# Batch 1's queries turned by VectorE and SyncE instead of TensorE, and the first unit of a fused attention-and-MLP kernel laid out anew

## The chip, the cores and the metric

The kernel runs on one core of a Trainium2 chip. The metric is the device time of one execution in microseconds. The kernel before took 898.84 us, the median of three runs (898.73, 898.84, 899.49). All data is float32.

## What is computed

Eight batches of attention, with eight heads, 576 queries and a head width of 64. Keys and values are averaged over groups of eight first, so each head has 72 keys. The result, 4608 tokens of 512 columns, goes through a two-layer network with a periodic activation between the layers:

```python
k_p = k.reshape(B, H, Sp, pool, D).mean(axis=3)          # pool = 8, Sp = 72
v_p = v.reshape(B, H, Sp, pool, D).mean(axis=3)
scores = scale * np.matmul(q, k_p.transpose(0, 1, 3, 2))
scores = scores - np.max(scores, axis=-1, keepdims=True)
attn = np.exp(scores)
attn = attn / (np.sum(attn, axis=-1, keepdims=True) + 1e-09)
x = np.matmul(attn, v_p)                                 # -> (4608, 512)
h = x @ w_in                                             # 512 x 2048
s = np.sin(alpha * h)
g = h + s * s / (alpha + 1e-09)
out = g @ w_out                                          # 2048 x 512
```

## The kernel before

**Stages.** The order of all instructions is written out by hand: what the program issues first on an engine runs first on it. First comes batch 0's attention (`first_batch`, L1105), which leaves the activations of the first 512 tokens in SBUF. Then the hidden layer runs in nine units `u` of 512 tokens (`hidden(u, extra)`, L835). Last comes the second layer (`outputs`, L1317, its products at L1383; the first of them start at 504.7 us, the hidden layer's last product at 510.9). The activated hidden values go from the one to the other through an internal DRAM tensor, `g_bridge`.

**A unit and its slots.** A unit has 28 slots: four groups J = 0 to 3 of output columns, each with seven products k = 0 to 6 (a Strassen scheme with seven products instead of eight, in the order 1, 5, 6, 2, 7, 3, 4). Slot number = 7J + k. One product is four matmuls of 128x256, which the trace shows as eight records at L866. Around each product the slot issues that group's share of the elementwise work: copies on ScalarE (L839), additions on VectorE (L838), sines and squares on ScalarE (`sin` L1028, `square` L1035), the last additions of the group before (`finish`, L1080) and the store of its result (`store_g`, L1091).

**Work hung on slots.** `carry(u)` (L1202) builds the list `extra`: `at(slot, f, ...)` appends a step to a slot. These steps are the attention of batch u+1, loads, and sums of weights, and they are issued between the unit's own instructions. Steps at "slot - 0.5" are issued at the start of the slot; those of a whole slot number at a fixed place inside it, mostly right ahead of its product. Unit 0 has a list of its own, because at that time batch 0's last tile is unfinished, w_in is still being loaded in four parts (`load_w_in_part`, L677; sums of each part by `combine_w_in`, L684), and q, k and v of batch 1 have just been requested.

**Batch 1's attention in unit 0, before.**
- `load_k` (L117) loads k of one half of the heads, with one run of 6 KB for each partition; `pool_rows` (L128) adds groups of eight on GpSimd (L132). `first_batch` issues k, then q of batch 1 (`load_q(1)`), then w_in's part 1; slot 2 issues w_in's parts 2 and 3.
- q: ScalarE puts heads into pairs (`pairs_q`, L88 to L98, slots 2 and 3). TensorE transposes five tiles of it, four transposes each (`q_t`, L282, transposes L290, slots 4, 4, 8, 8, 9), and VectorE or ScalarE copies them out of PSUM (L291). `k_t` (L274, slot 4) transposes the pooled k on TensorE.
- `two_scores` (L304, matmuls L318, slots 6 and 11): scores of query tiles 0 and 1, then of 2 and 3 with the last 64 rows. VectorE subtracts the row maximum (L341, L342), ScalarE takes the exponential (L366, slots 9, 9, 15, 15), `norm` (L369, slots 10, 10, 16, 16) has VectorE sum and invert the sums, and GpSimd multiply (L375).
- `turn` (L498, transposes L504, slots 13, 13, 19, 19): VectorE transposes the weights of attention in 32x32 blocks into the tile `tr`. `move` (L517, L524, slot 19) then carries bands of 32 partitions of `tr` to other partitions, into the tile `aM`, by DMA. There are four blocks of two halves of two transfers, 16 in all; before, SyncE issues the 12 of blocks 0 to 2 and ScalarE's queue the 4 of block 3.
- `all_values` (slot 26, matmuls L613) multiplies `aM` with the pooled values. Its first matmuls read the second halves of all four blocks of `aM`.

**Later batches' q, before.** `turn_q` (L216) has four parts. In parts 0 and 1 VectorE transposes q in 32x32 blocks into `tr` (L229, L234). In parts 2 and 3 SyncE issues eight moves each (L244), from bands of `tr` back into q's tile. For batch 2 the four parts stand in slots 23 to 26 of unit 0, and `tr` is the same buffer that the attention weights use. In the trace this tile is called `q` and the moves are `q<-tr`.

**Batch 0's last tile.** Its 64 rows finish in unit 0: `exp(4)` slot 9, `norm_rest` slot 13, `a_rest` (transposes) slot 21, `values_rest` (L626) slot 24.

**Queues.** SyncE issues nearly all transfers, in program order, and waits at each for what it needs. A DMA that waits holds back all later ones of SyncE. The end of J = 2's group in unit 0 is finished at slots 24 and 26 (`finish(Q, (0,))`, `finish(Q, (1,))`, `store_g`).

Of the kernel before, what the change touches and what calls it, by code (L numbers as in the profile page):

```python
# [13 lines left out]
F32 = mybir.dt.float32  # L14
# [26 lines left out]
class Kernel:  # L41
# [46 lines left out]
    def pairs_q(self, b, tiles):  # L88

        nc = self.nc  # L90
        if 0 in tiles:
            self.raw = self.q_views(self.qm[b])
            self.qm[b] = self.q_tile(1)
        x = self.qm[b][:].rearrange("p (t h e d) -> p t e h d", t=5, e=2, d=self.D)
        for t in tiles:
            n = P if t < 4 else 64
            raw = self.raw[0][:, :, t, :] if t < 4 else self.raw[1]
            nc.scalar.copy(out=x[:n, t], in_=raw.rearrange("p (e h) d -> p e h d", e=2))  # L98

    def load_q_rest(self, b, at=None):  # L100
        if b < 2:
            self.nc.sync.dma_start(out=self.q_views(self.qm[b])[1] if at is None else at, in_=self.q[b, :, 4 * P:, :].rearrange("h p d -> p h d"))
# [14 lines left out]
    def load_k(self, b, e):  # L117

        Sp, D, NP = self.Sp, self.D, self.NP
        m = Sp // 3  # L120
        t = self.kvp.tile([P, 2048], F32, name="kvin")[:NP * m, 0:3 * POOL * D]
        self.nc.sync.dma_start(out=t, in_=self.k[b, NP * e:NP * e + NP].rearrange("h (p x) d -> (h p) (x d)", x=3 * POOL))
        if b not in self.kp:
            self.kp[b] = self.ap.tile([NP * m, 3, 2, D], F32, name="kp")
        t, out = t.rearrange("p (j x) -> p j x", j=3), self.kp[b][:, :, e, :]
        self.pool_k[e] = lambda: self.pool_rows(t, out)
# [132 lines left out]
    def attention(self, b):  # L259
# [22 lines left out]
        def q_t(i, copy=nc.scalar.copy):  # L282

            n = rows[i]
            x = self.qm[b][:n].rearrange("p (t hp x) -> p t hp x", t=5, hp=NP)[:, i]
            if b not in self.qt:
                self.qt[b] = self.qt_view(self.q_tile(0))
            ps = self.abank([P, NP, P])
            for hp in range(NP):
                nc.tensor.transpose(ps[:, hp, :n], x[:, hp], self.ident[:n, :n])  # L290
            copy(out=self.qt_tiles(b)[:, i, :, :n], in_=ps[:, :, :n])  # L291

        def columns(hp, i):

            if b < 2:
# [73 lines left out]
        def norm(i):  # L369

            n = E(i).shape[1]
            sm = self.sm.tile([P, 12], F32, name="sm2")[:, 0:n]
            nc.vector.tensor_reduce(out=sm, in_=E(i, Sp + 1), axis=AX, op=OP.add)
            nc.vector.reciprocal(out=sm, in_=sm)
            nc.gpsimd.tensor_tensor(out=E(i), in0=E(i), in1=sm.unsqueeze(2).to_broadcast([P, n, Sp]), op=OP.mult)  # L375
# [150 lines left out]
        def to_x(ps, hp, t0, m, s0=0):  # L526

            while s0 < m:
# [5 lines left out]
                if t0 and b > 1:  # L534
# [8 lines left out]
        def value_parts(hp, rest):  # L543
# [14 lines left out]
            order = lambda x: x.rearrange("p a (t i) -> p t a i", i=32) if b == 1 else x  # L558
            at = lambda r, n, h: order(self.aM[r:r + n, :, 128 * h:128 * h + 128])
# [74 lines left out]
        return SimpleNamespace(**{f.__name__: f for f in (k_t, q_t, products, score, two_scores, two_shifts, exp, norm, new_a, turn, move, values, values_rest, all_values,  # L634
# [200 lines left out]
    def hidden(self, u, extra):  # L835
# [41 lines left out]
        for slot in range(7 * self.NJ):  # L877
# [6 lines left out]
            for f in extra[slot - 0.5]:  # L884
                f()

            if k == 0:
                Q = self.before = G
# [15 lines left out]
            elif k == 1:  # L904
                if not G.i1:
                    copy(G.b6[:], G.b1[:])
                if G.i5 and not G.i1:
                    self.last_sines(Q, 0)
                elif Q and not G.i1:
                    if end(J):  # L910
                        self.last_sines(Q, 2)
# [5 lines left out]
            elif k == 2:  # L917
                if Q and not G.i5 and not split(J):
# [20 lines left out]
            elif k == 3:  # L939
                late = J == 0 and busy  # L940
                if Q and not late and not G.i5 and not split(J):
# [11 lines left out]
                else:  # L953
# [11 lines left out]
                    extras()  # L965
                    product(G, 2, G.b1)
# [19 lines left out]
            elif k == 5:  # L986
                add(G.g[:, 1, :, 1], G.b7[:], G.p5[:])
                extras()
                if split(J):
                    self.finish(Q, (1,))  # L990
                    self.store_g(Q)
# [8 lines left out]
            else:  # L1000
# [3 lines left out]
                sin(G, 1, 1, G.g[:, 1, :, 1])  # L1004
# [100 lines left out]
    def first_batch(self):  # L1105
# [88 lines left out]
        self.load_w_in_part(0, ((2, 1, 0),))  # L1194
        for e in range(2):
            self.load_k(1, e)
            self.pool_k[e]()
        self.combine_w_in(0, (3,), nc.gpsimd)
        self.load_q(1)
        self.load_w_in_part(1)  # L1200

    def carry(self, u):  # L1202
# [6 lines left out]
        if u == 0:  # L1209
# [9 lines left out]
            at(2, self.load_w_in_part, 3)  # L1219
            at(2, self.pairs_q, 1, (0, 1))  # L1220
            at(3, self.pairs_q, 1, (2, 3, 4))
            at(4, self.combine_w_in, 1, (0, 1, 2, 3), self.nc.gpsimd)
            at(4, A.q_t, 0, self.nc.vector.tensor_copy)
            at(4, A.q_t, 1, self.nc.vector.tensor_copy)
            at(4, A.k_t)
            at(7, self.load_v, 1)
            at(7, lambda: self.pool_v())
            for i in range(2):
                at((6, 11)[i], A.two_scores, i)
            at(13, A.two_shifts)  # L1230
# [482 lines left out]
```

## Time and profile before

| | us |
|---|---|
| device time, median of 3 | 898.84 |
| profiled execution, first to last instruction (span) | 896.15 |
| hidden layer's last product starts (L866) | 510.86 |
| TensorE busy | 890.8 (99%) |
| VectorE busy | 682.9 (76%) |
| ScalarE busy | 438.6 (49%) |
| GpSimd busy | 249.2 (28%) |

The page gives the busy time of each engine over the span (PE is TensorE, DVE VectorE, ACT ScalarE, POOL GpSimd, SP SyncE; SPq marks a row of DMA issues by SyncE). Its second part cuts the span into 40 slices of 22.4 us, with busy shares in tenths; the two that matter here are the second and third (22 to 67 us), where nearly all of unit 0 lies:

```
POOL 6798443825338252434523000000000000000000
PEclk9999999999999999999999999999999999999999
DMA  9857957759586585648126243716435355164002
GB/s 269 244 158 206 244 147 212 187 164 254 139 ...
```

The granted TensorE clock is full in all slices. In the timeline a row is a run of equal instructions: its start, its length (for a pipelined engine from the first start to the last end), engine, line, operation, output <- inputs, shapes and count, and in brackets the idle time of the engine before it with what ended that. In unit 0 the rows of TensorE follow each other without such a bracket; slot 6 (the first scores) starts at 35.66, slot 11's scores at 47.14, slot 26's values at 76.32, and unit 1's first scores at 89.08.

### The profile page before, as it was taken

To read this page: it belongs to the slowest core of one execution; us is meant where nothing else is said; L and a number is where in the kernel's file an instruction comes from. 1 tells how busy PE (TensorE), PEld (TensorE's weight loads), DVE (VectorE), ACT (ScalarE), POOL (GpSimd) and SP (SyncE) were. 2 spreads that over 40 slices of the span, in tenths; PEclk is the share of its full clock that TensorE was granted. 3 is DMA by queue.
4 is the path that set the end of the run, shared out by engine and by line. 5 is a ranking of instruction groups with operands and counts; after the bars stand their busy time and mean duration, and the time that the engine had idled before them with its cause. 6 is when DMAs were issued, how large, how long until landed. Compare 5 with 4: busy or idle time off the path is not lost.

```text
span 896.2 us, 16276 instructions
## 1 busy us (share of the span) xinstructions
PE 890.8 (99%) x6274; PEld 813.9 (91%) x6274; DVE 682.9 (76%) x918; ACT 438.6 (49%) x1033; POOL 249.2 (28%) x265
## 2 busy tenths in 40 slices
PE   9999999999999999999999999999999999999998
PEld 6787888888888888888888999999999999999998
DVE  7786857768577675765677889898897896996885
ACT  6687776877768777687776711111111211111111
POOL 6798443825338252434523000000000000000000
PEclk9999999999999999999999999999999999999999
DMA  9857957759586585648126243716435355164002
GB/s 269 244 158 206 244 147 212 187 164 254 139 214 186 183 225 147 175 140 302 53 106 219 102 181 103 232 37 218 117 105 160 89 159 159 37 192 142 20 18 53
DMA packets 119533, 141.03 MB, mean 157 GB/s; under 512 B 45776, under 2 KB 86496, under 8 KB 119456
## 3 DMA queue, kind: packets, MB, share of 16 engines
q1 hardware_dynamic: 116288, 137.39, 52.6%
q10 hardware_dynamic: 3168, 2.61, 1.0%
q8 instruction: 50, 0.82, 0.4%
q14 instruction: 27, 0.22, 0.1%
HBM read 75.37 MB, written 47.19 MB: 137 GB/s over the span
## 4 chain that ended last, share of the span: by engine, by line
PE 99%; DVE 0%; POOL 0%; ACT 0%; issue 0%; DVEq 0%
PE PS L866 44%; PE PS L1383 43%; PE PS L1058 5%; PE PS L318 2%; PE PS L613 2%; PE PS L626 1%; PE PS L1126 0%; PE PS L571 0%; PE PS L290 0%; PE PS L425 0%; PE PS L279 0%; PE PS L479 0%; PE PS L569 0%; POOL tr L451 0%; PE PS L403 0%; PE PS L487 0%
## 5 line engine op out<-in xcount | busy, mean ns | idle before, releaser
L866 PE MATMUL PS<-home,a 128*128 128x256 f32 x1072 | 253.0, 381 | 0.1
L866 PEld LDWEIGHTS PS<-home,a 128*128 128x128 f32 x1072 | 198.4, 190 | 30.9 <-issue 4.6
L866 PE MATMUL PS<-home,as 128*128 128x256 f32 x736 | 177.2, 382 | 0.0
L866 PEld LDWEIGHTS PS<-home,as 128*128 128x128 f32 x736 | 134.5, 190 | 18.1 <-ACT PS L839 1.2
L1383 PE MATMUL PS<-s,wb 128*128 128x192 f32 x672 | 116.2, 326 | 0.0
L1035 ACT ACTIVATE s<-s,c 128x256 f32<-128x256 f32 (+1 forms) x236 | 115.5, 556 | 0.0
L1383 PEld LDWEIGHTS PS<-s,wb 128*128 128x128 f32 x672 | 110.4, 190 | 0.1
L132 POOL TENSOR_TENSOR kvin<-kvin 96x768 f32<-96x768 f32 (+3 forms) x42 | 73.4, 1747 | 69.9 <-DMA kvin<-in_v_dram 67.8
L838 DVE TENSOR_TENSOR h<-PS,p 128x512 f32<-128x512 f32 x72 | 49.2, 684 | 55.5 <-PE PS L866 35.2
L1554 ACT COPY PS<-PS 128x192 f32<-128x192 f32 x42 | 12.7, 303 | 146.2 <-PE PS L1383 130.0
L1028 ACT ACTIVATE s<-h,al 128x256 f32<-128x256 f32 x144 | 65.5, 509 | 32.6 <-DVE h L838 32.6
L1383 PE MATMUL PS<-r,wb 128*128 128x192 f32 x432 | 79.0, 326 | 0.0
L1383 PEld LDWEIGHTS PS<-r,wb 128*128 128x128 f32 x432 | 71.6, 190 | 0.0
L1383 PE MATMUL PS<-s,a 128*128 128x192 f32 x384 | 70.2, 326 | 0.0
L1028 ACT ACTIVATE s<-PS,al 128x256 f32<-128x256 f32 x144 | 60.0, 469 | 17.2 <-PE PS L866 16.5
L1383 PEld LDWEIGHTS PS<-s,a 128*128 128x128 f32 x384 | 63.7, 190 | 0.0
L1080 DVE TENSOR_TENSOR h<-PS,s 128x512 f32<-128x512 f32 x36 | 24.8, 689 | 48.6 <-ACT s L1035 48.6
L839 ACT COPY PS<-PS 128x512 f32<-128x512 f32 x72 | 41.5, 577 | 34.5 <-PE PS L866 26.7
L1080 DVE TENSOR_TENSOR h<-h,s 128x1024 f32<-128x1024 f32 x36 | 55.3, 1537 | 3.3 <-ACT s L1035 3.1
L1584 ACT COPY PS<-PS 128x192 f32<-128x192 f32 x42 | 12.7, 303 | 89.5 <-PE PS L1383 89.5
L1322 DVE TENSOR_TENSOR s<-r 128x768 f32<-128x768 f32 x54 | 51.4, 951 | 4.8 <-PE PS L1383 2.8
L1383 PE MATMUL PS<-s,we 128*128 128x192 f32 x288 | 52.7, 326 | 0.0
(244 smaller groups left out, 1401.4 us busy)
## 6 DMA issues: line engine op xcount, KB each, us to landing
g_bridge<-h SPq DMA_DIRECT2D x72, 512.0 KB
r<-g_bridge SPq DMA_DIRECT2D x15, 1536.0 KB
x<-g_bridge SPq DMA_DIRECT2D x8, 1536.0 KB
out_dram<-o SPq DMA_DIRECT2D x90, 96.0 KB
kvin<-in_k_dram SPq DMA_DIRECT2D x14, 576.0 KB
q<-in_q_dram SPq DMA_DIRECT2D x7, 1024.0 KB
kvin<-in_v_dram SPq DMA_DIRECT2D x14, 512.0 KB
aM<-tr SPq DMA_DIRECT2D x54, 92.0 KB
```

The lines of the kernel that those rows point to most:

```text
L132: self.nc.gpsimd.tensor_tensor(out=t[..., 0:w] if w > D else out, in0=t[..., 0:w], in1=t[..., w:2 * w], op=OP.add)
L318: nc.tensor.matmul(ps[e][r0 + r:r0 + r + q.shape[-1], h, :], q[s], kb[s, hp, :], start=True, stop=True)
L613: nc.tensor.matmul(o[r:r + 64], w, x, start=start and i < 2, stop=False, skip_group_check=True)
L838: add = lambda o, x, y: nc.vector.tensor_tensor(out=o, in0=x, in1=y, op=OP.add)
L839: copy = lambda o, x: nc.scalar.copy(out=o, in_=x)
L866: nc.tensor.matmul(ps[:, jj, :], self.A[p][:, kk, f * P:(f + 1) * P], x[:, kk, :], start=(start and n == 0), stop=(kk == 1), skip_group_ch ...
L1028: self.nc.scalar.activation(out=G.s[:, i, jj, j, :], in_=src[:, jj], func=AF.Sin, scale=self.al[:, f:f + 1])
L1035: self.nc.scalar.activation(out=x, in_=x, func=AF.Square, scale=self.c[:, f:f + 1])
L1058: nc.tensor.matmul(o, W[m][:, G.J - J0], X[m], start=start and n == 0, stop=True, skip_group_check=True)
L1080: add = lambda o, x, y: self.nc.vector.tensor_tensor(out=o, in0=x, in1=y, op=OP.add)
L1322: tt = lambda o, x, y, op: nc.vector.tensor_tensor(out=o, in0=x, in1=y, op=op)
L1383: nc.tensor.matmul(out, W[:, J // 2, J % 2, :], A[:, J, :], start=(start and J == 0), stop=(J == self.NJ - 1), skip_group_check=True)
```

## The change

The change concerns unit 0 and what is issued right before it; later units change only in the number of runs by which k is loaded.

1. `pairs_q` and `q_t` are gone. Batch 1's q is loaded and turned as later batches' q is: `turn_q(1)` with parts 0 and 1 at slot 3, part 2 at slot 4, part 3 at slot 5. The special cases for batch 1 in `load_q_rest`, `columns`, `to_x` and `value_parts` go with it.
2. `load_k` loads three runs of 2 KB for each partition instead of one of 6 KB, with 2,560 bytes from one run to the next in SBUF.
3. In `first_batch`, `load_q(1)` is issued ahead of k of batch 1, and `combine_w_in(0, (3,))` ahead of both. w_in's part 3 is issued behind part 2 of `turn_q(1)`.
4. `norm` of tiles 0 and 1 multiplies on VectorE instead of GpSimd.
5. Steps of unit 0 move to other slots (the list in the diff), among them the scores from slots 6 and 11 to 10 and 12, the pooling of v from 7 to 13, sums of w_in parts 2 and 3 from 8 and 17 to 6 and 7, `norm_rest` from 13 to 20, and `turn_q(2)` from 23, 24, 25, 26 to 25, 25, 26, 27.
6. `move` of the attention weights: ScalarE's queue issues only the first half of block 3 (2 transfers), SyncE the second half of block 3 and then blocks 0 to 2 (14 transfers).
7. In `hidden`, for unit 0: the last additions and the store of J = 1's and J = 2's groups are issued at slots 21 and 24, and J = 2's last sines at slot 22.

```diff
 def load_k(self, b, e):
-        t = self.kvp.tile([P, 2048], F32, name="kvin")[:NP * m, 0:3 * POOL * D]
-        self.nc.sync.dma_start(out=t, in_=self.k[b, NP * e:NP * e + NP].rearrange("h (p x) d -> (h p) (x d)", x=3 * POOL))
+        t = self.kvp.tile([P, 2048], F32, name="kvin")[:NP * m, 0:3 * 640].rearrange("p (j x) -> p j x", j=3)[..., 0:POOL * D]
+        self.nc.sync.dma_start(out=t, in_=self.k[b, NP * e:NP * e + NP].rearrange("h (p j x) d -> (h p) j (x d)", j=3, x=POOL))
...
-        def norm(i):
+        def norm(i, eng=nc.gpsimd):
...
-            nc.gpsimd.tensor_tensor(out=E(i), in0=E(i), in1=sm.unsqueeze(2).to_broadcast([P, n, Sp]), op=OP.mult)
+            eng.tensor_tensor(out=E(i), in0=E(i), in1=sm.unsqueeze(2).to_broadcast([P, n, Sp]), op=OP.mult)
...
-            order = lambda x: x.rearrange("p a (t i) -> p t a i", i=32) if b == 1 else x
-            at = lambda r, n, h: order(self.aM[r:r + n, :, 128 * h:128 * h + 128])
+            at = lambda r, n, h: self.aM[r:r + n, :, 128 * h:128 * h + 128]
...
 def hidden(self, u, extra):
-            for f in extra[slot - 0.5]:
+            for f in extra[slot - 0.25]:
...
             if k == 0:
+                if end(J):
+                    self.finish(before, (1,))
+                    self.store_g(before)
...
             elif k == 1:
...
+                for f in extra[slot + 0.5]:
+                    f()
...
                     if end(J):
+                        sin(Q, 1, 1, Q.g[:, 1, :, 1])
                         self.last_sines(Q, 2)
...
@@ k == 3 @@
                     extras()
+                    if end(J):
+                        self.finish(Q)
+                        self.store_g(Q)
                     product(G, 2, G.b1)
...
@@ k == 5 @@
-                if split(J):
-                    self.finish(Q, (1,))
-                    self.store_g(Q)
...
@@ k == 6 @@
-                sin(G, 1, 1, G.g[:, 1, :, 1])
+                if split(J):
+                    before = Q
+                else:
+                    sin(G, 1, 1, G.g[:, 1, :, 1])
...
 first_batch
+        self.combine_w_in(0, (3,), nc.gpsimd)
+        self.load_q(1)
         for e in range(2):
             self.load_k(1, e)
             self.pool_k[e]()
-        self.combine_w_in(0, (3,), nc.gpsimd)
-        self.load_q(1)
         self.load_w_in_part(1)
...
 carry, u == 0
-            at(2, self.load_w_in_part, 3)
-            at(2, self.pairs_q, 1, (0, 1))
-            at(3, self.pairs_q, 1, (2, 3, 4))
+            at(3, self.turn_q, 1, 0)
+            at(3, self.turn_q, 1, 1)
             at(4, self.combine_w_in, 1, (0, 1, 2, 3), self.nc.gpsimd)
-            at(4, A.q_t, 0, self.nc.vector.tensor_copy)
-            at(4, A.q_t, 1, self.nc.vector.tensor_copy)
-            at(4, A.k_t)
+            at(4, self.turn_q, 1, 2)
+            at(4, self.load_w_in_part, 3)
+            at(5, self.turn_q, 1, 3)
+            at(6, A.k_t)
+            at(6, self.combine_w_in, 2, (0, 1, 2, 3), self.nc.gpsimd)
+            at(7, self.combine_w_in, 3, (0, 1, 2, 3), self.nc.gpsimd)
             at(7, self.load_v, 1)
-            at(7, lambda: self.pool_v())
+            at(13, lambda: self.pool_v())
             for i in range(2):
-                at((6, 11)[i], A.two_scores, i)
+                at((10, 12)[i], A.two_scores, i)
             at(13, A.two_shifts)
-            for i in range(2, 5):
-                at((8, 8, 9)[i - 2], A.q_t, i)
-            at(9, A0.exp, 4)
-            at(13, A0.norm_rest)
+            at(12, A0.exp, 4)
             for i in range(4):
-                at((9, 9, 15, 15)[i], A.exp, i)
-                at((10, 10, 16, 16)[i], A.norm, i)
-                at((13, 13, 19, 19)[i], A.turn, i)
-            at(8, self.combine_w_in, 2, (0, 1, 2, 3), self.nc.gpsimd)
-            at(17, self.combine_w_in, 3, (0, 1), self.nc.gpsimd)
-            at(17, self.combine_w_in, 3, (2, 3), self.nc.gpsimd)
-            at(21, A0.a_rest)
-            at(24.5, lambda: A0.values_rest((5, 6, 7, (self.turn + 1) % 5)))
+                at((12, 12, 15, 15)[i], A.exp, i)
+                at((13, 13, 16, 16)[i], A.norm, i, nc.vector if i < 2 else nc.gpsimd)
+            for i in range(4):
+                at((15, 15, 19, 19)[i], A.turn, i)
+            at(20, A0.norm_rest)
+            at(24, A0.a_rest)
+            at(24.75, lambda: A0.values_rest((5, 6, 7, (self.turn + 1) % 5)))
...
-            at(19, A.move, range(3))
-            at(19, A.move, (3,), nc.scalar)
+            at(19.75, A.move, (3,), nc.scalar, (0,))
+            at(19.75, A.move, (3,), nc.sync, (1,))
+            at(19.75, A.move, range(3))
...
-                at(17, lambda e=e: self.pool_k[e]())
+                at(21, lambda e=e: self.pool_k[e]())
...
-                at(((turn, turn + 1) if u == 0 else (23, 24))[part] if part < 2 else turn + part, self.turn_q, u + 2, part)
+                at((25, 25, 26, 27)[part] if u == 0 else (23, 24, 24, 25)[part], self.turn_q, u + 2, part)
```

In later units `turn_q` keeps its slots.

More of the change, by code (lines that the diff above doesn't have):

```diff
@@ L86, in load_q_heads @@
                                in_=self.q[b, h0:h1, 0:4 * P, :].rearrange("h (p t) d -> p h (t d)", t=4))
[L88 to L98, printed above, removed]
     def load_q_rest(self, b, at=None):
-        if b < 2:
-            self.nc.sync.dma_start(out=self.q_views(self.qm[b])[1] if at is None else at, in_=self.q[b, :, 4 * P:, :].rearrange("h p d -> p h d"))
+        if b == 0:
+            self.nc.sync.dma_start(out=at, in_=self.q[b, :, 4 * P:, :].rearrange("h p d -> p h d"))
             return
@@ L120, in load_k @@
         m = Sp // 3
-        t = self.kvp.tile([P, 2048], F32, name="kvin")[:NP * m, 0:3 * POOL * D]
-        self.nc.sync.dma_start(out=t, in_=self.k[b, NP * e:NP * e + NP].rearrange("h (p x) d -> (h p) (x d)", x=3 * POOL))
+        t = self.kvp.tile([P, 2048], F32, name="kvin")[:NP * m, 0:3 * 640].rearrange("p (j x) -> p j x", j=3)[..., 0:POOL * D]
+        self.nc.sync.dma_start(out=t, in_=self.k[b, NP * e:NP * e + NP].rearrange("h (p j x) d -> (h p) j (x d)", j=3, x=POOL))
         if b not in self.kp:
             self.kp[b] = self.ap.tile([NP * m, 3, 2, D], F32, name="kp")
-        t, out = t.rearrange("p (j x) -> p j x", j=3), self.kp[b][:, :, e, :]
+        out = self.kp[b][:, :, e, :]
         self.pool_k[e] = lambda: self.pool_rows(t, out)
@@ L280, in k_t @@
             nc.vector.tensor_copy(out=kb[:].rearrange("p hp (x j) -> p j hp x", j=3), in_=ps.rearrange("p j (hp x) -> p j hp x", hp=NP))
[L282 to L291, printed above, removed]
         def columns(hp, i):
-            if b < 2:
+            if b == 0:
                 if i == 4:
@@ L533, in to_x @@
                 x = self.xT[u][:, hp, x0:x0 + w]
-                if t0 and b > 1:
+                if t0 and b:
                     x, y = (z.rearrange(f"p h ({n}) -> p h t i", t=2) for z, n in ((x, "i t"), (ps, "t i")))
@@ L632, in all_values @@
             to_x(rest, slice(0, 4), 512, 64)
-        return SimpleNamespace(**{f.__name__: f for f in (k_t, q_t, products, score, two_scores, two_shifts, exp, norm, new_a, turn, move, values, values_rest, all_values,
+        return SimpleNamespace(**{f.__name__: f for f in (k_t, products, score, two_scores, two_shifts, exp, norm, new_a, turn, move, values, values_rest, all_values,
                                                           k_head, k_last, q_head, rest_q, products_head, soft_shift, soft_exp, norm_head, norm_rest, a_head, a_rest)})
@@ L917, in hidden @@
             elif k == 2:
-                if Q and not G.i5 and not split(J):
+                if Q and not G.i5 and not split(J) and not end(J):
                     self.finish(Q)
@@ L940, in hidden @@
                 late = J == 0 and busy
-                if Q and not late and not G.i5 and not split(J):
+                if Q and not late and not G.i5 and not split(J) and not end(J):
                     self.store_g(Q)
```

## The prediction

> **What bounds the kernel now.** I read the page first: busy times, then the chain that ended last.
>
> ```profile
> span 896.2 us, 16276 instructions
> ...
> PE 890.8 (99%) x6274; PEld 813.9 (91%) x6274; DVE 682.9 (76%) x918; ACT 438.6 (49%) x1033; POOL 249.2 (28%) x265
> ...
> PE 99%; DVE 0%; POOL 0%; ACT 0%; issue 0%; DVEq 0%
> ```
>
> TensorE is the chain from end to end. So an edit can gain only what it takes off PE, and loses whatever makes PE wait. Next I read PE's timeline where batch 1's q is turned (columns: start us, us, engine, line, ...).
>
> ```profile
> 30.96 1.04 PE L290 MATMUL PS<-ident,q 128*128 128x128 f32 x8
> 31.84 0.41 PE L279 MATMUL PS<-ident,kp 96*128 96x96 f32 x3
> 32.09 1.92 PE L866 MATMUL PS<-home,a 128*128 128x256 f32 x8
> ...
> 40.38 1.06 PE L290 MATMUL PS<-ident,q 128*128 128x128 f32 x8
> 41.28 1.89 PE L866 MATMUL PS<-home,as 128*128 128x256 f32 x8
> 43.10 0.46 PE L290 MATMUL PS<-ident,q 64*128 64x64 f32 x4
> 43.49 1.99 PE L866 MATMUL PS<-home,as 128*128 128x256 f32 x8
> ```
>
> The reader sees groups that begin where the last one ends, with no bracketed idle time: PE has no wait to lose here. A product of eight L866 records takes 1.73 us of issue (the chain's 80 records at 48.67 take 17.46, less the last one's 0.38: 0.216 each).
>
> Then SyncE's queue, the end of unit 0 and VectorE's string before it, since these feed what is new.
>
> ```profile
> 65.52 7.88 SPq L524 DMA_DIRECT2D aM<-tr  x12
> ...
> 78.12 11.07 SPq L244 DMA_DIRECT2D q<-tr  x16
> ```
>
> ```profile
> 75.14 2.37 DVE L229 STREAM_TRANSPOSE tr<-q 128x1024 f32<-128x1024 f32 x2 [0.22 <-DMA aM<-tr]
> ...
> 76.32 0.65 PE L613 MATMUL PS<-aM,vm 64*64 64x512 f32 x6
> ```
>
> ```profile
> 52.36 0.69 DVE L838 TENSOR_TENSOR h<-PS,p 128x512 f32<-128x512 f32 x1 [0.96 <-PE PS L866]
> ...
> 57.76 0.71 DVE L504 STREAM_TRANSPOSE tr<-ex 128x512 f32<-128x512 f32 x1 [0.20 <-POOL ex L375]
> ...
> 61.66 0.69 DVE L1080 TENSOR_TENSOR h<-PS,s 128x512 f32<-128x512 f32 x1 [0.92 <-ACT s L1035]
> 62.72 0.69 DVE L838 TENSOR_TENSOR h<-PS,p 128x512 f32<-128x512 f32 x1 [0.37 <-PE PS L866]
> ...
> 65.51 1.90 DVE L1080 TENSOR_TENSOR h<-h,s 128x1024 f32<-128x1024 f32 x1
> ```
>
> A string of moves is paced by its issue: 7.88/12 = 0.66 us each (L524), 11.07/16 = 0.69 (L244). Issue of the last aM move ends at 73.40 and VectorE, which waits for it, starts at 75.14: 1.74 from issue to use. The values that read aM start at 76.32, so that string has 1.18 us to spare.
>
> **Taken off PE.** The two groups of eight transposes cost 31.84-30.96 = 0.88 and 41.28-40.38 = 0.90. The four of 64 rows: the product from 41.28 would end at 43.01, the next starts at 43.49 (0.48), and runs 1.83 to 45.32 instead of 1.73 (0.10). Together 2.36 us. The three k transposes (0.25) and both groups of scores only move. ScalarE loses the copies L98 (1.14+1.66 in the timeline) and L291 (1.33), VectorE two copies of 1.29 together; none was on the chain, so these bring nothing.
>
> **Added: the q moves, wait 1, at slot 12.** VectorE turns q behind L833, which ends at 30.57 (29.89+0.68). Two transposes and the rest took 75.14 to 78.10, 2.96. So 33.53 if nothing holds VectorE; up to 1.8 later if it must first let one of GpSimd's k additions end (L132, 96x768, mean 1.81), since those now run then; I put 0.65 for that: 34.2. SyncE holds still until then, with w_in part 3, v, and q of batch 2 behind it. Then eight moves (5.3 at 0.66), four w_in loads (0.42 each between the issue rows of 0.38 at L85 and 0.46 at L682: 1.7), eight moves (5.3), 1.74 to use: 48.2. PE by its own pace: 30.96, six products and k_t to the first scores (10.6), these with the change of tile (1.26), two products (3.46) is 46.3; 0.7 us into the second scores (32 of their 80 records and the change of tile) the last tile's moves are needed: 47.0. Wait 1.2. Bounds: 0 (33.53, and 0.59 a move, the median of the issues in L244's rows: then they land before PE wants them) and 2.8 (35.3, 0.69 a move). The first scores need the eighth move at 41.2 and come at 41.6: no wait.
>
> **Added: VectorE's string and two more moves, wait 2, at slot 26.** From the add at 52.36 to the last aM transpose at 65.51 VectorE now takes 13.15 us, 1.49 of it waits (0.20, 0.92, 0.37) and 1.03 the rest's sums (55.62 to 56.65), which go behind the string. That leaves 10.63. In come the sums and reciprocals of tiles 0 and 1 (47.02 to 48.80, 1.78) and their two multiplications from GpSimd: 128x576, between L833's 0.68 for 128x512 and L342's 0.76 from PSUM: 1.5. Now 13.9, or 14.3 with 0.4 for a busy GpSimd, so 1.15 later. The third block's half and one more half: SyncE issues 14 moves, not 12 (ScalarE 2, not 4): 1.31. Less the 1.18 to spare: wait 1.3. Bounds: 0.1 (13.9, and 14 moves at 0.6, 8.4) and 3.2 (each multiplication stands behind one GpSimd operation of 1.15, which is the mean of L375's 128x576). Wait 1 delays this string's start as much as PE, so the two add. The same lateness makes PE wait some 0.3 at slot 20 (its add ended 0.84 before the product that needs the bank); that lies inside wait 2.
>
> [...]
>
> **Put at nothing, with the cover.** k behind q: the page's slices move 302 GB/s at the most and 244 in the second, so q's 1.18 MB put k's landing (22.62, where GpSimd stops waiting) back by 3.9 to 4.8; the two poolings of 8.4 (22.62 to 31.03) then end at 34.9 to 35.8, and PE wants k at 34.4. That is a wait of up to 1.5, but it comes off wait 1, which is tied to SyncE and not to PE: nothing in the sum. 2 KB pieces may quicken k by 1 us; the later batches' k lands far ahead of need. GpSimd's w_in sums come before v, whose pooling ends near 58 and is used at 74. ScalarE's exps and two table loads (1.28 each) stand before the copy for slot 16, which I get 0.1 before its product; any wait 1 widens that. Batch 2's q: transposes wait for the aM moves, then 2.96, 5.3 and 1.74 end 10.0 after slot 26's start; the scores came 12.76 after it (89.08).
>
> **Sum.** 896.15 - 2.36 + 1.2 + 1.3 = 896.3; the run's median 898.84 is 2.69 over the profiled span, so 899.0.
>
> **Rivals.** (A) Both waits are hidden: 898.84-2.36 = 896.5. For it: PE's gain is certain, VectorE is 76% busy and SyncE idles from 50 to 65. Against: both strings are serial and short of room by over 1 us in rows.
> (B) Slower: VectorE stands behind GpSimd on their way to SBUF. Place: L833 and the two multiplications.
>
> ```profile
> 42.79 4.56 POOL L132 TENSOR_TENSOR kvin<-kvin 128x1024 f32<-128x1024 f32 x2 [4.85 <-DMA kvin<-in_v_dram]
> ...
> 43.23 3.00 DVE L1080 TENSOR_TENSOR h<-h,s 128x1024 f32<-128x1024 f32 x1
> ```
>
> The same add takes 1.28 at 88.94; here it lasts until GpSimd's first addition is over and 1.28 more. At full price waits 1 and 2 are 2.8 and 3.2: 898.84-2.36+6.0 = 902.5. It decides (over 900.6) once blocked time passes what I put in (1.05) by 1.6. For it: in the new order GpSimd pools k and v just then. Against: three full hits must coincide. [...]
> (C) Wait 1 is absorbed by k's lateness or quick moves and only wait 2 stays: 897.8, still no change.
>
> **Chances.** A run tells 0.2% (1.8 us) from nothing. Forecast 0.35 and C 0.15, both inside 897.04 to 900.64, which is the likeliest one's own range: same 0.50. A or near it: faster 0.26, since both low bounds lie at or by it. B: slower 0.24. Range 896.4 to 901.6, from A to most of B.
>
> **What would show it.** In the profile after: no L290; about 2.4 us fewer PE busy; a PE gap before the second scores ended by DMA q<-tr; one before the first values of batch 1 ended by DMA aM<-tr; SyncE issuing 14 aM moves in 9.2 us; multiplications on VectorE over 0.8 us where GpSimd adds beside them. I am wrong if neither gap is there, or a gap over 1 us stands elsewhere (k's transposes, slot 16 or 20, the scores of batch 2).

## The result, and the profile after

The changed kernel takes 902.93 us (median of 4 runs, 902.16 to 903.51) against 899.15 of the kernel before on the same chip (4 runs): ratio 1.0042, 95% interval 1.0028 to 1.0056. It is slower by 3.8 us, and lies above the range that was given (up to 901.6).

The page of the changed kernel, profiled in its quickest run (902.16 us): span, busy times, and shares of the chain that ended last. Line numbers are now those of the changed kernel (L838 is L814, L866 is L842, L318 is L295, L279 is L267, L613 is L589, L524 is L501, L1080 is L1065, L375 is L352, L132 is L120).

```profile
span 900.4 us, 16254 instructions
...
PE 889.6 (99%) x6254; PEld 812.6 (90%) x6254; DVE 685.1 (76%) x921; ACT 435.1 (48%) x1025; POOL 247.0 (27%) x263
...
PE 93%; DMA 3%; SPq 2%; DVE 1%; POOL 1%; issue 0%; DVEq 0%; POOLq 0%
```

TensorE is busy for 1.2 us less than before; the prediction's sign was about 2.4, for the removed transposes. From unit 0's first product to unit 1's first scores it is 1.5 less, behind that 0.6 more. And the chain is no longer TensorE's alone. TensorE's waits, in total, times, and the longest:

```profile
PE PS L842 <- DVE h L814: 2.3, 1, 2.3
PE PS L267 <- POOL kp L120: 1.1, 1, 1.1
...
PE PS L589 <- DMA aM<-tr: 0.9, 1, 0.9
```

All three stand in unit 0: k at slot 6, an addition of VectorE at slot 20, batch 1's values at slot 26. None is in the same list of the kernel before. VectorE's and GpSimd's rows of the timeline between 52 and 68 us show where the largest comes from:

```profile
52.15 0.69 DVE L814 TENSOR_TENSOR h<-PS,p 128x512 f32<-128x512 f32 x1 [0.96 <-PE PS L842]
...
56.43 0.76 DVE L352 TENSOR_TENSOR ex<-ex,sm 128x576 f32<-128x576 f32 x1
...
58.13 2.13 DVE L352 TENSOR_TENSOR ex<-ex,sm 128x576 f32<-128x576 f32 x1
...
63.85 0.63 DVE L1065 TENSOR_TENSOR h<-PS,s 128x512 f32<-128x512 f32 x1
65.80 0.69 DVE L814 TENSOR_TENSOR h<-PS,p 128x512 f32<-128x512 f32 x1 [1.32 <-DMA g_bridge<-h]
...
67.24 0.71 DVE L481 STREAM_TRANSPOSE tr<-ex 128x512 f32<-128x512 f32 x1
```
```profile
57.28 4.12 POOL L120 TENSOR_TENSOR kvin<-kvin 128x1024 f32<-128x1024 f32 x2 [4.26 <-DMA kvin<-in_v_dram]
...
64.47 2.74 POOL L352 TENSOR_TENSOR ex<-ex,sm 128x576 f32<-128x576 f32 x2
```

Two things in it were not in the forecast. VectorE's addition at 65.80, which opens slot 20 to TensorE, waits 1.32 us for a store: it writes into the buffer `h` that J = 0's group was kept in, and that group's store to `g_bridge` has only just landed. And GpSimd sits 4.26 us until v lands, pools it until 64.47, and only then multiplies tiles 2 and 3 (to 67.21), which VectorE's last transposes read: the one at 67.24 starts just behind, without a listed wait. Besides, the multiplication at 58.13 takes 2.13 us beside GpSimd's first addition of v (57.28), 0.76 without it. SyncE's rows (start, length, number of issues) say why v and the store are late:

```profile
34.26 5.03 SPq L232 DMA_DIRECT2D q<-tr  x8
39.33 2.14 SPq L658 DMA_DIRECT2D a<-in_moe_w_in_dram  x4
41.52 6.09 SPq L232 DMA_DIRECT2D q<-tr  x8
47.71 1.35 SPq L129 DMA_DIRECT2D kvin<-in_v_dram  x2
...
52.03 0.38 SPq L85 DMA_DIRECT2D q<-in_q_dram  x1
52.46 1.79 SPq L94 DMA_DIRECT2D q<-in_q_dram  x2
56.85 0.90 SPq L1079 DMA_DIRECT2D g_bridge<-h  x2
...
68.78 9.36 SPq L501 DMA_DIRECT2D aM<-tr  x14
```

The sixteen q moves, with w_in's part 3 between them, hold SyncE from 34.26 to 47.6. Behind them stand v (issued from 32.70 before), batch 2's q and the store (46.25 before, 56.85 now; its issue also waits until v's second load, eight transfers ahead, has landed at 56.79: both have semaphore 106 in the trace, and SyncE's list of waits has 2.5 us for it). The store lands at 65.67.

Where the 4.2 us between the two spans lie: 0.67 ahead of unit 0's first product (19.74 instead of 19.07), in which TensorE's instructions are the same but the loads stand in another order. This start lay between 18.94 and 21.72 in the kernels below, which share that part, so chance alone is as large; but it lay later than 19.07 in 15 of 16 profiles, so that the new order costs something here is not ruled out. 2.89 between that product and unit 1's first scores, called the stretch from here on: 72.90 (19.74 to 92.64) instead of 70.01 (19.07 to 89.08). And 0.67 behind it, taken up below. The stretch leaves out the start and the later units, so theories are told apart by it. But each kernel has one profile, so the spread of its stretch is not known, and where the whole times say otherwise, that is said too.

### The profile page after: what moved, and what is told of

Read it like the earlier page. It is cut to its first block, busy times and chain, and to the rows that moved or that the text cites. A ratio compares the mean times of both kernels' runs of the same rounds, so it can differ in the third digit from the quotient of the medians.

```text
span 900.4 us, 16254 instructions
## 1 busy us (share of the span) xinstructions
PE 889.6 (99%) x6254; PEld 812.6 (90%) x6254; DVE 685.1 (76%) x921; ACT 435.1 (48%) x1025; POOL 247.0 (27%) x263
## 3 DMA queue, kind: packets, MB, share of 16 engines
q10 hardware_dynamic: 3072, 2.42, 0.9%
## 4 chain that ended last, share of the span: by engine, by line
PE 93%; DMA 3%; SPq 2%; DVE 1%; POOL 1%; issue 0%; DVEq 0%; POOLq 0%
PE PS L1367 42%; PE PS L842 40%; PE PS L1043 5%; PE PS L295 2%; PE PS L589 2%; DMA kvin<-in_k_dram 1%; DMA g_bridge<-h 1%; SPq L501 1%; PE PS L602 1%; DMA h<-in_v_dram 1%; POOL kvin L120 1%; SPq L94 0%; PE PS L267 0%; DMA aM<-tr 0%; DVE h L814 0%
## 5 line engine op out<-in xcount | busy, mean ns | idle before, releaser
L842 PE MATMUL PS<-home,a 128*128 128x256 f32 x1072 | 252.5, 381 | 2.4 <-DVE h L814 2.3
L842 PEld LDWEIGHTS PS<-home,a 128*128 128x128 f32 x1072 | 198.4, 190 | 33.7 <-issue 4.5
L842 PE MATMUL PS<-home,as 128*128 128x256 f32 x736 | 177.0, 382 | 0.0
L842 PEld LDWEIGHTS PS<-home,as 128*128 128x128 f32 x736 | 134.6, 190 | 18.1 <-ACT PS L815 1.2
L120 POOL TENSOR_TENSOR kvin<-kvin 96x768 f32<-96x768 f32 (+3 forms) x42 | 75.1, 1787 | 74.5 <-DMA kvin<-in_v_dram 69.5
L814 DVE TENSOR_TENSOR h<-PS,p 128x512 f32<-128x512 f32 x72 | 49.2, 683 | 54.5 <-PE PS L842 34.5
L1367 PE MATMUL PS<-s,a 128*128 128x192 f32 x384 | 70.3, 326 | 0.0
L1065 DVE TENSOR_TENSOR h<-PS,s 128x512 f32<-128x512 f32 x36 | 24.7, 686 | 48.2 <-ACT s L1020 48.2
L1065 DVE TENSOR_TENSOR h<-h,s 128x1024 f32<-128x1024 f32 x36 | 53.9, 1497 | 3.3 <-ACT s L1020 3.1
```

Source lines behind the costliest of these rows:

```text
L120: self.nc.gpsimd.tensor_tensor(out=t[..., 0:w] if w > D else out, in0=t[..., 0:w], in1=t[..., w:2 * w], op=OP.add)
L814: add = lambda o, x, y: nc.vector.tensor_tensor(out=o, in0=x, in1=y, op=OP.add)
L842: nc.tensor.matmul(ps[:, jj, :], self.A[p][:, kk, f * P:(f + 1) * P], x[:, kk, :], start=(start and n == 0), stop=(kk == 1), skip_group_ch ...
L1065: add = lambda o, x, y: self.nc.vector.tensor_tensor(out=o, in0=x, in1=y, op=OP.add)
L1367: nc.tensor.matmul(out, W[:, J // 2, J % 2, :], A[:, J, :], start=(start and J == 0), stop=(J == self.NJ - 1), skip_group_check=True)
```

## The experiments

The queue theory: SyncE's order makes v and the store late, and these set VectorE's last transposes and both late waits; a wait of TensorE ahead of them only uses up time. The rivals: the store alone; VectorE's own string of sums and multiplications (the forecast's wait 2); each wait by itself. The kernel before, run beside them, took 898.89 to 899.15. The waits are TensorE's, as in the list above (for k, for q moves at the scores, at slot 20, before the values).

| run | us | ratio to before, 95% | stretch | k | q | slot 20 | values |
|---|---|---|---|---|---|---|---|
| changed kernel | 902.93 | 1.0042 (1.0028-1.0056) | 72.90 | 1.1 | | 2.3 | 0.9 |
| e1 | 901.61 | 1.0029 (1.0018-1.0040) | 72.16 | | 1.0 | 1.4 | 0.8 |
| e2 | 902.14 | 1.0037 (1.0025-1.0049) | 73.33 | 1.1 | | 2.9 | |
| e3 | 901.40 | 1.0025 (1.0014-1.0036) | 71.52 | 1.1 | | 1.3 | 0.9 |
| e4 | 902.16 | 1.0039 (1.0025-1.0053) | 73.63 | 1.1 | | 2.6 | |
| e5 | 901.98 | 1.0032 (1.0020-1.0045) | 72.93 | | 0.7 | 2.6 | |
| e6 | 906.61 | 1.0082 (1.0067-1.0097) | 78.06 | 1.2 | | 5.5 | |
| e7 | 906.15 | 1.0077 (1.0062-1.0092) | 76.83 | | | 5.5 | |
| e8 | 907.42 | 1.0090 (1.0075-1.0105) | 78.57 | | | 9.1 | |
| e9 | 899.86 | 1.0008 (0.9999-1.0018) | 70.89 | | | | 0.5 |
| e10 | 899.75 | 1.0008 (0.9998-1.0017) | 70.02 | 1.0 | | | 0.9 |
| e11 | 899.21 | 1.0002 (0.9993-1.0011) | 69.04 | | | | 0.9 |
| e12 | 903.44 | 1.0047 (1.0032-1.0062) | 73.44 | | | 4.0 | |
| e13 | 898.22 | 0.9996 (0.9987-1.0005) | 68.60 | | | 0.3 | |
| e14 | 900.54 | 1.0017 (1.0008-1.0027) | 71.79 | 1.1 | | 1.6 | 0.9 |
| e15 | 899.37 | 1.0006 (0.9997-1.0015) | 70.43 | 1.1 | | | 0.9 |

**e1 to e3: the store and GpSimd's order, alone and together.**

```diff
 e1, e3
-            at(9, self.load_q, 2)
+            at(11, self.load_q, 2)
 e2, e3
-            at(13, lambda: self.pool_v())
+            at(17, lambda: self.pool_v())
```


> The changed kernel with load_q(2) at slot 11 instead of 9, so that SyncE issues the store of J = 0's group ahead of batch 2's q (1.18 MB). Queue theory: in the changed kernel VectorE's addition at 65.80 waits for that store to land (65.67), and GpSimd's multiplications for tiles 2 and 3, behind the pooling of v, end at 67.21; both are late because SyncE issued sixteen q moves first, and both end at the same time. Taking away the one alone shortens the wait at slot 20 from 2.3 to about 1.1 us and lengthens the one at slot 26 from 0.9 to about 2.2: the last transposes for aM still end near 68.7 and the time stays 902.9. Store theory (the store alone sets the end): both waits shrink, 901.6. String theory (VectorE's own added sums and multiplications are late, the store only looks like the cause): no wait changes, 902.9.

> The changed kernel with the second part of the pooling of v (the 64 last rows) at slot 17 instead of 13, so that GpSimd multiplies tiles 2 and 3 first. Queue theory: GpSimd's multiplications end near 65.4 instead of 67.21, but VectorE still waits for the store until 65.80 and ends its transposes near 68.1: both waits as they are, within 0.6 us: 902.3 to 902.9. Rival (GpSimd's pooling sets the end): slot 26's wait is gone, 901.9. String theory: 902.9.

> Both edits of the two runs before at once. Queue theory: the addition at slot 19 starts when VectorE is free, 64.5, and the transposes end 1.3 us earlier (67.4): the wait at slot 20 falls from 2.3 to about 1.1, that at slot 26 stays near 0.9, 901.6. Store theory: the same as with the store alone, 901.6. String theory: 902.9.

With both edits the stretch fell by 1.38, as the queue theory had it (1.3); in e3 the store had landed at 60.46, and VectorE's addition followed its neighbour without a gap. e1 alone gained 0.74 (1.3 in time), more than the theory's nothing, and its time is the store theory's 901.6. But v landed 1.1 us earlier too (55.65 instead of 56.79), so both limits moved, and e1 does not tell the two theories apart. That was probably not the edit: v's second load landed 8.4 us after its issue in the changed kernel and 8.7 in e4, but 7.2 to 7.4 in e2, e5 and e14, where batch 2's q also stands behind it. In e1 k happened to come in time, and the second scores waited 1.0 for `q<-tr` instead. e2 did not shorten the wait for the store (1.36 on VectorE). Its stretch grew by 0.43, because TensorE ran slowly after its 2.9 us wait (5.17 us for two products, 3.72 in the changed kernel; see the last section); that also hid the wait before the values, which the rival had forecast to go.

**e4: aM's moves as before; e5: k transposed later.**

```diff
 e4
-            at(19.75, A.move, (3,), nc.scalar, (0,))
-            at(19.75, A.move, (3,), nc.sync, (1,))
+            at(19.75, A.move, (3,), nc.scalar)
 e5
-            at(6, A.k_t)
+            at(8, A.k_t)
```


> The changed kernel with the moves of block 3 of aM all on ScalarE's queue, as before the change: 12 on SyncE, 4 on ScalarE. All theories: the last move is issued 1.3 us earlier (76.3 instead of 77.6), lands near 78.4, and the wait before the values (0.9) is gone: 901.9. If issue from two queues does not run side by side, 902.9.

> The changed kernel with k_t at slot 8 instead of 6. Queue theory (SyncE's late queue sets the end of unit 0; TensorE's earlier waits only use up time that it would wait later): the wait for GpSimd's k (1.1) goes, a wait for DMA q<-tr of about 1.0 at the second scores takes its place, the later waits stay; from unit 0's first product to unit 1's first scores 72.9 us as in the changed kernel, 902.9 in all. Rival (each wait costs by itself): 1.2 less, 901.7.

In e5 the wait for k went, 0.7 for q's moves and a longer wait at slot 20 took its place: slot 20's product starts 46.49 us behind unit 0's first one, 46.80 in the changed kernel, so of 1.1 only 0.3 was gained there. The stretch stayed at 72.93, with TensorE running slowly behind slot 20 (5.41 us for two products). The time does not settle it: 901.98 is nearer to the rival's 901.7 than to 902.9, and the intervals overlap. In e4 the wait before the values went, and the time (902.16) came near the expected 901.9, but the stretch did not fall; here too TensorE ran slowly behind slot 20 (5.41). What the two moves cost was left to e13.

**e6 to e8: a mended queue that was worse.** VectorE turns q at slot 2; eight q moves go ahead of w_in's part 2 and eight behind it, v ahead of part 3.

```diff
+            at(2, self.turn_q, 1, 0)
+            at(2, self.turn_q, 1, 1)
             at(2, A0.values, (2, 3), (2, 1), 1, 1)
...
+            at(2, self.turn_q, 1, 2)
             at(2, self.load_w_in_part, 2)
+            at(3, self.turn_q, 1, 3)
...
+            at(5, self.load_v, 1)
+            at(6, self.load_w_in_part, 3)
             at(7, self.combine_w_in, 3, (0, 1, 2, 3), self.nc.gpsimd)
+            at(7, lambda: self.pool_vm())
...
 e7: and at(8, A.k_t)
 e8: and norms 0 to 3 on GpSimd, at(17, lambda: self.pool_v())
```
`pool_vm` is the pooling of v's first part, taken out of `load_v`; batch 2's q is loaded at slot 11.


> The changed kernel with the queue mended: VectorE turns batch 1's q at the start of slot 2, right after it lands, SyncE issues the q moves ahead of w_in's parts 2 and 3 and v ahead of part 3, and q of batch 2 behind the store of J = 0's group (slot 11). Queue theory: v lands near 50 instead of 57 and the store near 53 instead of 65.7; neither is waited for. What is left is VectorE's string: the wait at slot 20 falls from 2.3 to about 1.2, the one at slot 26 stays near 0.9, k's wait (1.1) stays: the stretch from unit 0's first product to unit 1's first scores falls from 72.9 to 71.6, the time to 901.6. Rival (the string alone is late): 72.9, 902.9. If the early turn delays TensorE at slot 2 by up to 1 us, add that.

> The run before with k_t at slot 8. Queue theory: now nothing on SyncE's queue is late, so k's wait (1.1) is gone without another in its place, and VectorE's string, which starts from TensorE's products, moves with it: 1.2 less than the run before (stretch 70.4, time 900.4). Rival: the wait comes back at slot 12 or 20, no less than the run before (901.6).

> The run before with all four multiplications on GpSimd, behind the first part of the pooling of v, whose second part goes behind them (slot 17). VectorE's string loses its two multiplications (0.76 and 2.13 in the changed kernel, the longer one stood behind GpSimd). String and queue theory together: the waits at slot 20 and 26 both go; the stretch is that of before less TensorE's 2.36 us, 67.7, the time 896.5 to 897.2. If GpSimd's multiplications come too late for VectorE's transposes: waits as in the run before, 900.4 or more.

All three missed by 5 us and more. GpSimd's and VectorE's timeline of e6:

```profile
56.53 1.27 POOL L666 TENSOR_TENSOR as<-a,a 128x512 f32<-128x512 f32 x1 [7.71 <-DMA a<-in_moe_w_in_dram]
```
```profile
70.44 0.71 DVE L483 STREAM_TRANSPOSE tr<-ex 128x512 f32<-128x512 f32 x1 [5.47 <-POOL ex L354]
```

v was early (50.4), but w_in's part 3, now the last load, landed at 56.9; GpSimd sums it ahead of v's pooling and of its multiplications, so it stood still for 7.71 us and VectorE then for 5.47. These runs bear on the same point from the other side: what stands last in SyncE's queue sets the end, through GpSimd's fixed order. e7's k_t gave 1.23 of the stretch without a wait in its place, as expected, though only 0.46 of the time.

**e9: the old way for q in the new layout.** q's pairs and twenty transposes are put back (`pairs_q` at slots 2 and 3, `q_t` at 4, 4, 8, 8, 9), w_in's part 3 at slot 2; the rest of the change stays.


> The changed kernel's layout with the old way for batch 1's q: pairs on ScalarE, twenty transposes on TensorE (tiles 0 and 1 at slot 4, 2 to 4 at slots 8, 8, 9), no q moves, and w_in's part 3 loaded right behind part 2. It tells the moves from the rest of the change. Moves theory (SyncE's sixteen q moves make v and the store late, and with them all that follows): without them v lands near 43 and the store near 53; the waits at slots 20 and 26 go, the stretch from unit 0's first product to unit 1's first scores is that of before, 70.0, the time 898.9. String theory (the rest of the layout is slow by itself: two multiplications on VectorE, two more aM moves on SyncE, k behind q): the waits at slot 20 (1.2) and 26 (0.9) stay, 72.3 and 901.2 or more.

The waits for k and at slot 20 are gone, 0.5 before the values is left. The stretch is 70.89, 2.01 less than the changed kernel's, although TensorE has its 2.36 us of transposes back. So the moves, and what they push back, cost 4.4 us of stretch, and the rest of the layout about 0.9; 70.0 was expected. The string theory (72.3 or more) falls: VectorE's string is not late by itself.

**e10, e14, e11, e13: all loads ahead of the moves.**

```diff
 e10, e11, e13, e14
             at(2, self.load_w_in_part, 2)
+            at(2, self.load_w_in_part, 3)
...
-            at(4, self.load_w_in_part, 3)
 e10, e11, e13: at(11, self.load_q, 2)
 e11, e13: at(8, A.k_t), at(17, lambda: self.pool_v())
 e13: at(19.75, A.move, (3,), nc.scalar), no second half on nc.sync
```


> The changed kernel with w_in's part 3 loaded right behind part 2, ahead of all q moves, and batch 2's q behind the store (slot 11). Moves theory: SyncE issues the sixteen moves without a break from 34.3 to 44.5 and v from 44.5, 3 us earlier than in the changed kernel; v lands near 52 and the store near 55. Left are k's wait (1.1) and VectorE's string at slot 20 (1.2) and 26 (0.9): stretch 71.5, time 901.5. If the moves land late because they now stand behind w_in's part 3 in the DMA rings, a wait at the first scores takes this back: 72.9.

> The changed kernel with w_in's part 3 loaded right behind part 2, batch 2's q still ahead of the store (slot 9). If the order of w_in's part 3 is what counts (q moves without a break, v and the store 2 us earlier): the store lands near 62, before VectorE asks for it at 63; stretch 70.0 to 70.5, time 899.8 to 900.2. If batch 2's q in front of the store counts: the store lands at 64 or later, wait at slot 20 about 1.5 to 2: stretch 71.5 to 72, time 901.3.

> The run before with k_t at slot 8 and GpSimd's multiplications for tiles 2 and 3 ahead of the last rows of v (slot 17). Moves theory: nothing that SyncE issues is waited for any more, so k's wait goes and no other takes its place: stretch 70.3, time 900.3. Rival (another wait takes it back): 71.5.

> The kernel of e11 with 12 aM moves on SyncE and 4 on ScalarE, as before the change. Moves theory: the wait before batch 1's values (0.9) is made of the two moves more on SyncE's queue (1.3); with them gone the last move lands near 74.6, ahead of TensorE: stretch 68.1 us, time 898.2. Rival (VectorE's string holds it): stretch 69.0, 899.2.

e10 has all that the change has, with two groups of loads in another place, and lies 3.2 us under it, not to be told from the kernel before. SyncE's and VectorE's timeline of e10:

```profile
20.00 14.00 SPq L658 DMA_DIRECT2D a<-in_moe_w_in_dram  x12
35.20 10.43 SPq L232 DMA_DIRECT2D q<-tr  x16
45.72 1.34 SPq L129 DMA_DIRECT2D kvin<-in_v_dram  x2
...
50.04 0.90 SPq L1079 DMA_DIRECT2D g_bridge<-h  x2
```
```profile
56.25 0.92 DVE L352 TENSOR_TENSOR ex<-ex,sm 128x576 f32<-128x576 f32 x1
...
58.11 0.81 DVE L352 TENSOR_TENSOR ex<-ex,sm 128x576 f32<-128x576 f32 x1
...
62.50 0.63 DVE L1065 TENSOR_TENSOR h<-PS,s 128x512 f32<-128x512 f32 x1
63.05 0.68 DVE L814 TENSOR_TENSOR h<-PS,p 128x512 f32<-128x512 f32 x1
```

w_in's part 3 is issued in the time that SyncE otherwise waits for VectorE's turn (30.95 to 34.26 in the changed kernel); the moves run without a break, v is issued 2 us and the store 6.8 us earlier, and VectorE has no gap left ahead of L814, which starts 2.75 us earlier. The wait for the store (1.32) is gone, and the two multiplications take 0.92 and 0.81 instead of 0.76 and 2.13. Why, the first additions of v show, in e3 and then in e10:

```profile
55.70 4.11 POOL L120 TENSOR_TENSOR kvin<-kvin 128x1024 f32<-128x1024 f32 x2 [2.79 <-DMA kvin<-in_v_dram]
56.24 2.42 DVE L352 TENSOR_TENSOR ex<-ex,sm 128x576 f32<-128x576 f32 x1
```
```profile
54.19 4.10 POOL L120 TENSOR_TENSOR kvin<-kvin 128x1024 f32<-128x1024 f32 x2 [1.32 <-DMA kvin<-in_v_dram]
```

GpSimd's row holds two additions, and the first ends at 58.05 in e3, at 56.55 in e10. VectorE's multiplication beside it ends 0.61 to 0.62 us later, in these two as in the changed kernel (59.65 and 60.26) and, where GpSimd's is one of w_in's sums, in e6 (57.80 and 58.41). In e1, e3 and e13, where VectorE does not wait for the store, TensorE's wait at slot 20 is that multiplication's length less 1.15 (1.45 for 2.60, 1.28 for 2.42, 0.29 for 1.44); where it took 0.92 to 1.29 (e10, e15, e11) no wait is listed. So what e3 left at slot 20 is the blocked multiplication, and how long it is blocked depends on when v lands. The theories had not seen this: e10 was expected at 71.5, with that wait still there.

In the stretch neither edit does it alone: part 3 gives 1.11 (e14, as expected if batch 2's q in front of the store counts), batch 2's q 0.74 (e1), the two together 2.88 (72.90 to 70.02). The times do not show this: 2.4, 1.3 and 3.2 us, and e14's profile was one of its slower runs (901.53), with moves that took 12.23 us instead of 10.43. That the two edits together undo the loss is shown; how they share it is not.

In e11 k's wait went and 0.98 of stretch with it (70.3 was expected). In e13 the wait before the values went as well: the last move is issued at 73.64 and not 73.76 although its string began 0.4 later. The time is the expected 898.2; the expected stretch of 68.1 was missed by 0.5, since 0.3 at slot 20 and 0.2 at a copy of ScalarE appeared. What issuing two more of the moves from ScalarE's queue saves here, with 88 and 92 KB in a move, is the 0.9 us wait, of which 0.44 shows in the stretch. e13 is the best version found, and it is not measurably faster than the kernel before (0.9987 to 1.0005).

**e12: all multiplications on GpSimd, again; e15: k in one run of 6 KB.** e12 is e13 with v's first part pooled ahead of w_in's third sums, two of those behind the multiplications of tiles 0 and 1. e15 is e10 with `load_k` as it was.


> The run before with all multiplications on GpSimd: v's first part pooled ahead of w_in's third sums, of which two go behind the multiplications of tiles 0 and 1; and 12 aM moves on SyncE, 4 on ScalarE. VectorE's string is 2.3 us shorter, the last move 1.3 earlier: no wait at slots 20 and 26, the stretch that of before less 2.36, 67.7, the time 896.5 to 897.2. If v lands after 53, GpSimd's multiplications come late: 69.5 to 71, 899 to 901.

> The kernel of e10 with k loaded in one run of 6 KB for each partition. If the 2 KB pieces quicken k: k lands up to 1 us later, TensorE's wait for it grows from 1.0 to about 2, stretch 71.0, time 900.7. If they do nothing: 70.0, 899.75. If they slow k: 69.5, 899.2.

e12 missed both values it was given. v landed at 53.1 and GpSimd's queue was too long for the early multiplications: VectorE waited 5.63 us for them. In e15 k's first half landed 9.5 us after its issue (17.89 to 27.39), with the 2 KB pieces 9.4 (18.67 to 28.08, changed kernel) and 9.8 (18.66 to 28.47, e10): the pieces do nothing that can be told.

## Why the prediction was wrong, step by step

- **Off PE, 2.36.** Right. From unit 0's first product to slot 12's the changed kernel takes 30.37 us (19.74 to 50.11), the kernel before 31.36 (19.07 to 50.43); that is 0.99 less, after k's wait took back 1.25 (from 35.21, the end of the product before, to 36.46): 2.24 without it.
- **Wait 1, 1.2 at the second scores.** The sum was right, the place wrong: the wait is k's. The prediction had said that k's wait comes off wait 1; in e1 and e5 k's wait went and one for q's moves came (1.0 and 0.7). The moves began at 34.26 (34.2 forecast).
- **Wait 2, 1.3 before the values.** This is the step that failed: TensorE waits 2.51 at slot 20 (63.81 to 66.54 less one record's 0.22) and 1.04 before the values (78.58 to 79.84 less the same), 3.55 in all. The term that was too small is VectorE's string. From the addition at 52.15 to the first aM move at 68.78 it takes 16.63 us; before, from 52.36 to 65.52, 13.16. That is 3.47 later, where 1.15 was put in. The work itself came out as forecast (13.94 without wait and blocking, 13.9 forecast). What was missing is the wait for the store, 1.32, and most of the blocking, 1.37 where 0.4 was put in. The 14 moves took 9.36 (9.2 forecast).
- **Why these two were missed.** The prediction named what stands behind the moves on SyncE as "w_in part 3, v, and q of batch 2", and stopped there. The store of J = 0's group stands there too, and its reader is VectorE's addition at slot 19, by way of a buffer. And v was put at nothing ("pooling ends near 58 and is used at 74"): its pooling began at 57.28, so that its first addition fell on VectorE's multiplication, and GpSimd's own multiplications stand behind it. In e3 the wait for the store is gone and the blocking left, in e10 both are gone. That GpSimd's multiplications would have held VectorE next is likely in the changed kernel (0.03 us apart) and shown in e6.
- **Slot 20 "inside wait 2".** Put at 0.3; it was the larger part, and e1 to e14 show it moving with the store and the blocked multiplication.
- **The prediction's own signs.** L290 is gone, and the gap before batch 1's values and one multiplication over 0.8 us came; the gap before the second scores did not, and gaps over 1 us at k's transposes and at slot 20 were its sign of being wrong.
- **Rival B, 902.5.** Near in number, which is partly luck: only one of its three hits came (1.37). The blocking is real, though (2.13 us instead of 0.76 for the second multiplication of the changed kernel), and it fits the rival's place: in the kernel before, L1080's `h<-h,s`, which does not read PSUM, takes 1.17 to 3.00 us, its `h<-PS,s`, which does, 0.65 to 0.69, although a GpSimd operation runs when 18 of the 36 start. e10 is as quick as the kernel before because its multiplications are hardly blocked (0.92 and 0.81), not because blocking costs nothing.
- **The sum's frame.** 2.69 was added for what lies around the span. All later kernels have 1.7 to 1.9 between span and time (902.16 and 900.4 here), so the profiled execution of before was probably about 0.9 us quicker than its timed runs.
- **Unforeseen, 0.67 in later units.** With q moved it is 0.25 to 0.8, in e9 0.02. Its cause stays open.

## What to carry to other kernels

When transfers are added to a queue, list everything that the queue issues behind them, stores too, and for each who next reads or overwrites that buffer. Issue loads that wait for nothing in the time in which the queue would wait for an engine, ahead of transfers that are paced by their issue (here 0.65 us a move, 10.43 for sixteen in e10). Shortening a wait early in a stage may gain little while a later wait of the stage is tied to another queue's clock (0.3 of 1.1 at slot 20 in e5). Where a VectorE operation can be blocked by GpSimd, as here (2.13 us instead of 0.76), ask what starts GpSimd just then: here it is a load's landing, and with it a queue's order.

## What the runs showed of the hardware that was not expected

TensorE's granted clock was 1.00 behind a wait of 2.35 us, and 0.58 from 68 to 72 us behind one of 2.63 (e4, e5). Windows of 65 to 68 and 68 to 72 us (busy times of PE, PEld, DVE, ACT, POOL with counts, then granted clock, DMA share, GB/s), the changed kernel with its wait of 2.35, then e2 with 2.89:

```profile
65.00:68.00 3.00, 1.46 (x7) 1.30 (x8) 2.20 (x5) 0.00 (x0) 2.20 (x2) 1.00 0.64 182
68.00:72.00 4.00, 4.00 (x20) 3.54 (x19) 3.83 (x10) 0.67 (x2) 1.15 (x1) 1.00 0.48 120
```
```profile
65.00:68.00 3.00, 1.93 (x5) 1.57 (x6) 2.68 (x8) 0.00 (x0) 2.27 (x5) 0.60 0.21 73
68.00:72.00 4.00, 4.00 (x18) 3.46 (x17) 3.29 (x7) 0.72 (x2) 1.68 (x2) 0.87 0.56 138
```

The clock is 1.00 throughout in the first and 0.60, then 0.87 in the second. The two products behind the wait took 3.72 us after waits of 1.28 (e3) and 2.35, but 5.41 after 2.63 (e4, e5), 5.17 after 2.89 (e2), 5.41 after 3.98 (e12) and 6.03 after 5.48 (e6, 15 of their 16 records); in these five one of the windows that they lie in has a clock of 0.57 to 0.60. A little more waiting cost up to 1.7 us more, and then hid the wait before the values. No run has a wait between 2.35 and 2.63 there, and what lowers the clock is not shown. Two of the changed kernel's other runs had a mean clock of 0.997 and 0.998 and took 0.7 and 1.4 us more than the profiled one (0.999); but the fourth, at 1.000, took 0.8 more, so that the clock made the difference is not shown.
